# A decode-attention kernel: q's projection as a loop over the chunks of x, and eight unread matmuls in TensorE's waits

## The chip, the cores and the metric

The kernel runs on one core of a Trainium2 chip. The metric is the device time of one execution in microseconds (us); beside it stands the time of a profiled execution, whose trace is what the prediction reads. A core has TensorE (PE in the profile; its weight loads are PEld), VectorE (DVE), ScalarE (ACT), GpSimd (POOL) and SyncE (SP), each with a program of its own, and 16 DMA engines that all queues share. The engines wait for each other through semaphores, which are counters.

## The reference

Two attention layers A and B of one shape, each for one new token, and their outputs side by side. For each:

```python
q = (x @ wq).reshape(B, Sq, H, Dh).transpose(0, 2, 1, 3)     # x 1x1x512, wq 512x4096, H=32, Dh=128
scores = einsum("bhqd,bhkd->bhqk", q, k_cache) * Dh ** -0.5  # k_cache 1x32x8192x128, bf16
p = softmax(scores)
o = einsum("bhqk,bhkd->bhqd", p, v_cache)                    # v_cache 1x32x8192x128
out = o.transpose(0, 2, 1, 3).reshape(1, 1, 4096) @ wo       # wo 4096x512
```

K and V of both layers are 64 MiB each, 256 MiB together; with the weights 285 MB are read once.

## The kernel before, in words

**The rounds.** The 64 heads of both layers are worked on in N = 16 groups of G = 4 heads, one group a round. A group's K or V is 8 MiB. It is laid on 128 partitions, 32 partitions for each head and 256 positions on each partition. K has two slots in SBUF (`kn`), V has one (`vn`).

**SyncE issues all the large loads in one written order**, each behind a wait of its own: both `wq` (into the room of V, line 187), K of rounds 0 and 1 (line 197), V of round 0 (line 205), K of round 2, V of round 1, K of round 3 and so on. `load_v(0)` waits on `c_q` until all of q's matmuls have read `wq` (line 203). `load_v(n)` waits until round n-1 has read V (line 201). `load_k(n)` waits until TensorE has read K of round n-2 (line 196, semaphore `c_red`). The last two V come in two parts of 192 and 64 positions (line 207), with a semaphore for each. At the end come `wo` of A, the first half of `wo` of B, the last V, and the other half of `wo` of B in six pieces (`load_wob`, line 220).

**The projection q (lines 409 to 423).** `x` lies on the partitions in C = 4 chunks, and q is wanted on all partitions at once, so a chunk of `x`, repeated over 128 columns, is the stationary operand and 512 columns of `wq` move. Eight turns of a loop `r` make two groups each, `j` = 0 and 1, with one PSUM tile (`yps[0]`, `yps[1]`) for each. For a group TensorE waits until ScalarE has copied that tile's former content (`c_qa`), then issues four matmuls in a row, one for each chunk, and raises `c_q` once behind the fourth. ScalarE waits for that one (`w_q`) and copies four 32x128 pieces into `qmem` (line 372), while TensorE makes the other group.

**A round.** VectorE multiplies K by q in place, in two halves (line 280, `muls`); it begins only when all of q has been copied (line 273). TensorE sums over part of the head dimension with an identity matrix in four tiles (`scores`: a matmul of one element, line 430, that opens the tile, then a hardware loop of four turns with four matmuls each, line 436). VectorE sums the rest (line 308). Maximum, its spread and the exponentials follow on VectorE, TensorE and ScalarE (lines 313, 476, 478, 378, 383). When V has landed, 64 matmuls of 32x512 add up p times V in `acc` (line 492), and in the next round VectorE takes the diagonal out of `acc` (lines 285 and 288) and TensorE sums it over partitions (`total_of_group`, line 442).

**The end.** In the last two rounds the 64 matmuls wait a second time, ahead of the last 16, for the second part of V (`w_v2`, line 490). In the last round, `mid` (lines 447 to 467) multiplies what is known of the output by `wo`. Behind the rounds TensorE takes the pieces of `wo` of B as they land (line 506), with `total_of_group` for the last group ahead of the second piece; the sum is copied out by VectorE (line 352) and ScalarE (line 386), and sent to HBM.

Of the kernel before, what the change touches and what calls it, by code (L numbers as in the profile page):

```python
# [11 lines left out]
P = 128  # L12
# [33 lines left out]
def bass_concat_heads__mha_block_cached__gqa_block_cached__decode_kernel(  # L46
# [19 lines left out]
    H, Sk, Dh = ks[0].shape[1:]  # L66
# [3 lines left out]
    C = D // P  # L70
    scale = float(Dh) ** -0.5

    G = 4
# [4 lines left out]
    N = NA * GA  # L78
# [16 lines left out]
    with ExitStack() as st:  # L95
# [8 lines left out]
        vn = sb("vn", [P, KS], BF16)  # L104
# [12 lines left out]
        xT = sb("xT", [P, NA * C], BF16)  # L117
# [66 lines left out]
        @block.sync  # L184
        def _(e):
            for a in range(NA):
                e.dma_start(vn[:, a * WQ:(a + 1) * WQ],
                            wqs[a].rearrange("(p c) n -> p (c n)", p=P)).then_inc(s_w[a], 16)

            def group(x, n):  # L190
                a, i = divmod(n, GA)
                return x[a][0, G * i:G * (i + 1)].rearrange("h (p t) d -> (h p) (t d)", p=HP)

            def load_k(n):
                if n >= 2:
                    e.wait_ge(c_red, RED * (n - 1))
                e.dma_start(kn[:, n % 2 * KS:(n % 2 + 1) * KS], group(ks, n)).then_inc(s_k[n % 2], 16)

            def load_v(n):
                if n:  # L200
                    e.wait_ge(c_pv, n + 1)
                else:
                    e.wait_ge(c_q, N)
                if n < N - 2:
                    e.dma_start(vn[:], group(vs, n)).then_inc(s_v, 16)
                else:
                    for t0, t1, s in ((0, VT, s_v), (VT, T, s_v2)):
                        e.dma_start(vn[:, t0 * Dh:t1 * Dh],  # L208
                                    group(vs, n)[:, t0 * Dh:t1 * Dh]).then_inc(s, 16)

            def load_wob(g):
                h0, n, rows = WOB[g]
                src = wos[1][h0 * Dh:(h0 + n) * Dh, :]
                dst = kn[:, WO + h0 * NOUT:WO + (h0 + n) * NOUT]
                if rows:
                    src = src.rearrange("(p j) n -> p (j n)", p=P)
                elif n > 1:
                    src = src.rearrange("(j p) n -> p j n", p=P)
                    dst = dst.rearrange("p (j n) -> p j n", j=n)
                e.dma_start(dst, src).then_inc(s_wob[g], 16)  # L220

            load_k(0)
            load_k(1)
            for n in range(N - 1):
                load_v(n)
                if n + 2 < N:
                    load_k(n + 2)
            e.wait_ge(c_red, RED * (N - 1))
            e.dma_start(kn[:, 0:WO], wos[0].rearrange("(p j) n -> p (j n)", p=P)).then_inc(s_woa, 16)
            load_wob(0)  # L230
            load_v(N - 1)
            for g in range(1, len(WOB)):
                load_wob(g)
            e.wait_ge(s_out, 16)
# [120 lines left out]
        @block.scalar  # L355
        def _(e):
            with once(e):
                for a in range(NA):
                    e.dma_start(xrow[a:a + 1, :], xs[a][0]).then_inc(s_x, 16)
                w_q = _Stepped(e, c_q, 1, 1)  # L360
                w_bc = _Stepped(e, c_bc, 1, 1)
                w_nb = _Stepped(e, c_nb, 1, 1)
                w_pv = _Stepped(e, c_pv, 1, 1)
                e.wait_ge(c_pv, 1)
                e.copy(xT[:].rearrange("p (a c) -> p c a", c=C),
                       misc[:, 0:C * NA].rearrange("p (c a) -> p c a", a=NA)).then_inc(c_qa, 2)
                with e.Fori(0, N // 2) as r:
                    for j in range(2):
                        w_q()
                        for h in range(G):  # L370
                            p = slice(h * HP, (h + 1) * HP)
                            i = e.copy(qflat[p, bass.ds(r * (2 * Dh) + j * Dh, Dh)],  # L372
                                       yps[j][p, h * Dh:(h + 1) * Dh])
                        i.then_inc(c_qa, 1)
                e.wait_ge(c_pool, NPOOL)
                with e.Fori(0, N):
                    w_bc()
                    e.activation(negb[:], bmp[:, 0:G], AF.Copy, scale=-scale).then_inc(c_nb, 1)  # L378
                    w_nb()
                    w_pv()  # L380
                    for h in range(G):
                        p = slice(h * HP, (h + 1) * HP)
                        e.activation(pt[p, 0:T, h], s_sb[p, :], AF.Exp, bias=negb[p, h:h + 1], scale=scale,  # L383
                                     accum_out=rsum[p, h:h + 1]).then_inc(c_p, 4)
                e.wait_ge(c_y, 2)
                e.copy(out_sb[:, NH:NOUT], yps[1][HP:HP + NA, 0:NH]).then_inc(c_ya, 1)
                e.wait_ge(c_yd, 2)
                e.wait_ge(c_ya, 1)
                e.dma_start(out[0].rearrange("o (a n) -> (o a) n", a=NA), out_sb[:]).then_inc(s_out, 16)
# [3 lines left out]
        def _(e):  # L393
            with once(e):
# [14 lines left out]
                with e.Fori(0, N // 2) as r:  # L409
                    with e.If(r == GA // 2):  # L410
                        e.wait_ge(s_w[1], 16)
                    a = r // (GA // 2)
                    w0 = r * (2 * G * Dh) + a * (WQ - H * Dh)
                    x0 = a * C
                    for j in range(2):
                        e.wait_ge(c_qa, by_tile)
                        e.reg_add(by_tile, by_tile, 1)
                        for c in range(C):
                            i = e.matmul(  # L419
                                yps[j][:], xT[:, bass.ds(x0 + c, 1)].broadcast_to([P, P]),  # L420
                                vn[:, bass.ds(w0 + (c * H * Dh + j * G * Dh), G * Dh)],
                                start=(c == 0), stop=(c == C - 1))
                        i.then_inc(c_q, 1)

                def scores(tile):
                    e.wait_ge(c_mul, by_tile)
# [20 lines left out]
                def mid():  # L447
# [17 lines left out]
                    for b in range(2):  # L465
                        e.matmul(yps[1][b * HP:b * HP + NA, 0:NH], sel16[:, 0, 0:NA],
                                 yc[:, b * NH:(b + 1) * NH], start=True, stop=False, skip_group_check=True)

                with e.Fori(0, N) as r:
                    with e.Fori(0, NB // 2):  # L470
                        for tile in range(2):
                            scores(tile)
                            e.reg_add(koff, koff, HT * Dh - Dh)
                    e.reg_alu(koff, koff, 2 * KS - 1, op=ALU.bitwise_and)
                    e.wait_ge(c_g, by_round)
                    e.matmul(mtp[0:1, 0:P], m1[:], ident_f[:], start=True, stop=True).then_inc(c_gx, 1)  # L476
                    e.wait_ge(c_gm, by_round)
                    e.matmul(bmp[:, 0:G], ones_f[0:1, :], gm[:], start=True, stop=True).then_inc(c_bc, 1)  # L478
                    with e.If(r > 0):
                        total_of_group()  # L480
                    with e.If(r == N - 1):
                        mid()
                    e.wait_ge(c_p, by_round)
                    e.matmul(misc[:, 0:G], ones_f[:], rsum[:], start=True, stop=True)  # L484
                    e.wait_ge(s_v, by_round)
                    e.reg_add(by_round, by_round, 16)
                    for g in range(NG):
                        if g * W == VT:
                            with e.If(r >= N - 2):
                                w_v2()  # L490
                        k = g % G * HP
                        m = e.matmul(acc[k:k + HP, :], ptf[:, g * W * G:g * W * G + HP],  # L492
                                     vn[:, g * W * Dh:(g + 1) * W * Dh], start=(g < G), stop=(g >= NG - G))
                    m.then_inc(c_pv, 1)


                for g in range(1, len(WOB)):
                    h0, n, rows = WOB[g]
                    if g == 2:
                        total_of_group()  # L500
                    e.wait_ge(s_wob[g], 16)
                    if h0 == H - G:
                        e.wait_ge(c_o, N + 1)
                    for h in range(h0, h0 + n):
                        for b in range(2):
                            m = e.matmul(yps[1][b * HP:b * HP + NA, 0:NH], o2[:, H + h, :],  # L506
                                         wo_rows(H + h)[:, b * NH:(b + 1) * NH], start=False,
                                         stop=(h == H - 1), skip_group_check=True)
# [29 lines left out]
```

## Time and profile before

| | |
|---|---|
| runs | 665.43, 665.60, 665.69 us; median 665.6 |
| profiled execution | 665.7 us, span 664.2 us (1.5 us lie around the span) |
| busy time | PE 385.1 us, DVE 363.3 us, ACT 76.0 us |
| mean granted TensorE clock | 0.784 |
| read from HBM | 285.21 MB, 429 GB/s over the span |

A row of the timeline has start, duration, engine, source line, operation, output <- inputs, shape, count, and in brackets the idle time ahead with what ended it. SPq and ACTq are the queues that issue transfers. A chain row has start, duration and what the time went to; "DMA vn<-..." there is the time between a transfer's issue and its landing. PEclk is the granted clock of TensorE, where 1.00 is full speed.

### The profile page before, as it was taken

What the parts mean: (1) busy time and instruction counts of PE and PEld (TensorE: products, weight loads), DVE (VectorE), ACT (ScalarE), POOL (GpSimd) and SP (SyncE); (2) the same over time, 40 slices, a digit from 0 to 9 for tenths busy, and PEclk for the clock granted to TensorE, in tenths of its full rate; (3) what the DMA queues carried; (4) which work ended last, traced back from release to release, by engine and by line L of the source; (5) the groups of instructions that cost most, each with busy time, mean ns of one, the idle gap of its engine ahead of it and who ended that gap; (6) DMA issues with size and microseconds to landing.
All of it is one profiled execution on the core that took longest, in us unless ns stands there. A gap on an engine that the chain in (4) does not pass through costs nothing.

```text
span 664.2 us, 7946 instructions
## 1 busy us (share of the span) xinstructions
PE 385.1 (58%) x2398; PEld 169.4 (25%) x2398; DVE 363.3 (55%) x250; ACT 76.0 (11%) x211; POOL 2.3 (0%) x12
## 2 busy tenths in 40 slices
PE   1719392854819275481928548192854819285776
PEld 0203141322304132230413223041322304132332
DVE  1046757548292654829275482927547292754821
ACT  1710202020010202001020200102020010202020
POOL 1000000000000000000000000000000000000000
PEclk9968787786958778695877869597786959778789
DMA  9999999999999999999989999999999999989998
GB/s 379 442 442 442 442 442 391 430 442 442 442 442 399 422 442 442 442 442 442 442 387 434 442 442 442 442 442 414 406 442 442 442 442 442 434 387 458 426 413 344
DMA packets 6472, 285.22 MB, mean 429 GB/s; under 512 B 708, under 2 KB 1224, under 8 KB 1608
## 3 DMA queue, kind: packets, MB, share of 16 engines
q1 hardware_dynamic: 6464, 285.22, 99.5%
q10 hardware_dynamic: 8, 0.00, 0.0%
HBM read 285.21 MB, written 0.00 MB: 429 GB/s over the span
## 4 chain that ended last, share of the span: by engine, by line
DMA 82%; PE 15%; issue 1%; ACT 1%; SPq 0%; ACTq 0%; DVE 0%
DMA vn<-in_A_v_cache_dram 41%; DMA vn<-in_B_v_cache_dram 34%; PE acc L492 13%; DMA kn<-in_B_wo_dram 5%; PE yps L419 2%; DMA vn<-in_A_wq_dram 2%; ACT qmem L372 1%; SPq L220 0%; PE yps L506 0%; SPq L208 0%; ACTq L43 0%; ACTq L372 0%; DVE out_sb L352 0%
## 5 line engine op out<-in xcount | busy, mean ns | idle before, releaser
L280 DVE TENSOR_TENSOR kn<-kn,qmem 128x16384 bf16<-128x16384 bf16 x32 | 276.7, 8688 | 49.6 <-DMA kn<-in_A_k_cache_dram 37.1
L436 PE MATMUL rps<-kn,ident 128*128 x1024 | 236.2, 383 | 0.4
L492 PE MATMUL acc<-vn,pt 128*32 128x512 bf16 x1024 | 92.0, 537 | 153.5 <-DMA vn<-in_A_v_cache_dram 80.4
L308 DVE TENSOR_REDUCE s_sb<-rps 128x64 f32<-128x512 f32 x64 | 44.3, 692 | 166.8 <-PE rps L436 166.8
L436 PEld LDWEIGHTS rps<-kn,ident 128*128 128x128 bf16 x1024 | 96.5, 98 | 110.4 <-issue 22.3
L492 PEld LDWEIGHTS acc<-vn,pt 128*32 128x32 bf16 x1024 | 38.4, 129 | 200.6 <-issue 194.3
L378 ACT ACTIVATE negb<-bmp 128x4 f32<-128x4 f32 x16 | 2.8, 173 | 547.3 <-PE bmp L478 547.3
L383 ACT ACTIVATE pt<-s_sb,negb 32x256 bf16<-32x256 f32 x64 | 54.9, 858 | 4.3 <-ACT negb L378 3.0
L484 PE MATMUL misc<-rsum,ones_f 128*128 128x4 f32 x32 | 9.2, 358 | 56.4 <-ACT pt L383 56.4
L285 DVE TENSOR_SCALAR om<-acc,msk 128x128 f32<-128x128 f32 x16 | 5.6, 350 | 41.8 <-PE acc L492 41.8
L484 PEld LDWEIGHTS misc<-rsum,ones_f 128*128 128x128 f32 x32 | 7.8, 304 | 58.2 <-ACT pt L383 57.7
L419 PE MATMUL yps<-vn,xT 128*128 x64 | 17.4, 422 | 8.5 <-ACT qmem L372 4.4
L288 DVE SCALAR_TENSOR_TENSOR om<-acc,msk,om 128x128 f32<-128x128 f32 x48 | 16.8, 351 | 5.9
L430 PE MATMUL rps<-ones_bf,zrow 1*128 1x1 bf16 x64 | 11.0, 172 | 15.6 <-DVE kn L280 15.4
L476 PE MATMUL mtp<-ident_f,m 128*1 128x128 f32 x32 | 6.1, 270 | 22.6 <-DVE m L313 22.6
L372 ACT CAST qmem<-yps 32x128 f32 x64 | 16.4, 256 | 9.4 <-PE yps L419 8.6
L430 PEld LDWEIGHTS rps<-ones_bf,zrow 1*128 1x128 bf16 x64 | 5.8, 91 | 42.8 <-issue 42.8
L383 ACT ACTIVATION_READ_ACCUMULATOR pt<-s_sb,negb 32x1 f32 x64 | 15.9, 248 | 0.0
L419 PEld LDWEIGHTS yps<-vn,xT 128*128 x64 | 6.6, 103 | 18.9 <-issue 16.0
L478 PE MATMUL bmp<-gm,ones_f 1*128 1x4 f32 x32 | 6.1, 258 | 7.3 <-DVE gm L315 7.3
L297 DVE TENSOR_TENSOR oD<-mtp,rinv 128x4 f32 x15 | 2.4, 162 | 13.6 <-PE mtp L442 13.6
L315 DVE TENSOR_REDUCE gm<-mtp 1x4 f32<-1x128 f32 x16 | 4.5, 279 | 8.9 <-PE mtp L476 8.9
(56 smaller groups left out, 50.9 us busy)
## 6 DMA issues: line engine op xcount, KB each, us to landing
vn<-in_B_v_cache_dram SPq DMA_DIRECT2D x2, 6144.0 KB, 28.0
vn<-in_A_wq_dram SPq DMA_DIRECT2D x1, 4096.0 KB, 12.2
vn<-in_B_wq_dram SPq DMA_DIRECT2D x1, 4096.0 KB, 21.4
vn<-in_B_v_cache_dram SPq DMA_DIRECT2D x2, 2048.0 KB, 32.5
kn<-in_A_wo_dram SPq DMA_DIRECT2D x1, 4096.0 KB, 27.8
kn<-in_B_wo_dram SPq DMA_DIRECT2D x1, 2048.0 KB, 32.3
kn<-in_B_wo_dram SPq DMA_DIRECT2D x3, 512.0 KB, 34.1
kn<-in_B_wo_dram SPq DMA_DIRECT2D x1, 256.0 KB, 35.2
```

The lines of the kernel that those rows point to most:

```text
L280: e.tensor_tensor(k, k, qflat[:, bass.ds(q, Dh)].unsqueeze(1).broadcast_to([P, HM, Dh]), ALU.mult).then_inc(c_mul, 2)
L288: e.scalar_tensor_tensor(om[t % 2][:], acc[:, t * Dh:(t + 1) * Dh], msk[:, t:t + 1], om[(t + 1) % 2][:], ALU.mult, ALU.add).then_inc(*((c_ ...
L308: e.tensor_reduce(s_sb[:, h * HT:(h + 1) * HT], rps[:, h % 2, :].rearrange("p (t d) -> p t d", d=DW), AX.X, ALU.add).then_inc(c_sr, 1)
L372: i = e.copy(qflat[p, bass.ds(r * (2 * Dh) + j * Dh, Dh)], yps[j][p, h * Dh:(h + 1) * Dh])
L383: e.activation(pt[p, 0:T, h], s_sb[p, :], AF.Exp, bias=negb[p, h:h + 1], scale=scale, accum_out=rsum[p, h:h + 1]).then_inc(c_p, 4)
L419: i = e.matmul(yps[j][:], xT[:, bass.ds(x0 + c, 1)].broadcast_to([P, P]), vn[:, bass.ds(w0 + (c * H * Dh + j * G * Dh), G * Dh)], start=(c ...
L430: e.matmul(rps[:, tile, 0:1], zrow[:], ones_bf[0:1, 0:1], start=True, stop=False, skip_group_check=True)
L436: m = e.matmul(ro, ident[:], src, start=False, stop=False, skip_group_check=True)
L476: e.matmul(mtp[0:1, 0:P], m1[:], ident_f[:], start=True, stop=True).then_inc(c_gx, 1)
L478: e.matmul(bmp[:, 0:G], ones_f[0:1, :], gm[:], start=True, stop=True).then_inc(c_bc, 1)
L484: e.matmul(misc[:, 0:G], ones_f[:], rsum[:], start=True, stop=True)
L492: m = e.matmul(acc[k:k + HP, :], ptf[:, g * W * G:g * W * G + HP], vn[:, g * W * Dh:(g + 1) * W * Dh], start=(g < G), stop=(g >= NG - G))
```

## The change

Two things. **q's matmuls**: the four chunks no longer stand in a row for one group. First both tiles are waited for and opened with a matmul of one element that writes zeros (stationary `zrow`). Then a hardware loop over the four chunks issues one matmul for each of the two groups, each of which raises `c_q`. So `c_q` counts 64 instead of 16, group 0 is complete at the seventh of eight and group 1 at the eighth, and ScalarE and SyncE wait for these counts. **Eight matmuls that nobody reads**: `turn_over(n)` issues n matmuls of 128x128 by 128x512 into the scores tile `rps[:, 0]`, in a hardware loop. It stands with n = 5 ahead of the wait for the second part of V in each of the last two rounds, and with n = 3 ahead of the last `total_of_group`.

```diff
-                    e.wait_ge(c_q, N)
+                    e.wait_ge(c_q, N * C)
...
-                w_q = _Stepped(e, c_q, 1, 1)
+                w_q = _Stepped(e, c_q, 2 * C - 1, 2 * C)
+                w_q2 = _Stepped(e, c_q, 2 * C, 2 * C)
...
-                        w_q()
+                        (w_q, w_q2)[j]()
...
-                        for c in range(C):
-                            i = e.matmul(
-                                yps[j][:], xT[:, bass.ds(x0 + c, 1)].broadcast_to([P, P]),
-                                vn[:, bass.ds(w0 + (c * H * Dh + j * G * Dh), G * Dh)],
-                                start=(c == 0), stop=(c == C - 1))
-                        i.then_inc(c_q, 1)
+                        e.matmul(yps[j][:, 0:1], zrow[:], ones_bf[0:1, 0:1], start=True, stop=False,
+                                 skip_group_check=True)
+                    with e.Fori(0, C) as c:
+                        for j in range(2):
+                            e.matmul(yps[j][:], xT[:, bass.ds(x0 + c, 1)].broadcast_to([P, P]),
+                                     vn[:, bass.ds(w0 + c * (H * Dh) + j * G * Dh, G * Dh)],
+                                     start=False, stop=False, skip_group_check=True).then_inc(c_q, 1)
...
+                def turn_over(n):
+
+                    with e.Fori(0, n):
+                        e.matmul(rps[:, 0, :], ident[:], vn[:, 0:512], start=True, stop=True)
+
...
                             with e.If(r >= N - 2):
+                                turn_over(5)
                                 w_v2()
...
                     if g == 2:
+                        turn_over(3)
                         total_of_group()
```

## The prediction

> **What bounds the kernel now.** I read the page first, its DMA queues.
>
> ```profile
> span 664.2 us, 7946 instructions
> ...
> PE 385.1 (58%) x2398; PEld 169.4 (25%) x2398; DVE 363.3 (55%) x250; ACT 76.0 (11%) x211; POOL 2.3 (0%) x12
> ...
> q1 hardware_dynamic: 6464, 285.22, 99.5%
> ```
>
> The large loads keep the 16 DMA engines occupied for 99.5% of the span, while the busiest compute engine, TensorE, is busy for 385.1 of 664.2 us. Next I read the chain of work that ended last, in order of time. It runs through V alone, but its starts are landings of V, and these tell the pace.
>
> ```profile
> 35.61 45.11 DMA vn<-in_A_v_cache_dram
> 80.72 0.12 issue
> ...
> 119.42 0.12 issue
> ...
> 584.11 0.12 issue
> ...
> 626.38 35.17 DMA kn<-in_B_wo_dram
> 661.55 0.04 issue
> 661.59 0.64 PE yps L506 x6
> ...
> 662.59 0.41 DVE out_sb L352
> ```
>
> V of round 0 lands at 80.72 and V of round 1 at 119.42, 38.70 later; V of round 13 lands at 584.11, and (584.11 - 80.72) / 13 = 38.72 us a round: the pace is steady. Each round moves a K and a V, so 8 MiB take 19.36 us. The kernel is a single file of transfers from start to end, and only 1.5 us of compute stand behind the last landing (661.55 to 663.0). Hence the rule for this change: a delay of compute costs nothing while the file has work, and every microsecond in which the file runs dry is added to the end, since no later stage goes faster than the file.
>
> **The place where the file could run dry.** For that I read the timeline of the first round and two rows on the first load.
>
> ```profile
> 0.80 0.37 SPq L187 DMA_DIRECT2D vn<-in_A_wq_dram  x1
> ...
> 13.85 5.98 PE L419 MATMUL yps<-vn,xT 128*128 x16 [4.16 <-DMA vn<-in_A_wq_dram]
> ...
> 20.54 1.90 PE L419 MATMUL yps<-vn,xT 128*128 x8 [0.71 <-ACT qmem L372]
> ...
> 21.71 2.14 ACT L372 CAST qmem<-yps 32x128 f32 x8 [0.48 <-PE yps L419]
> ...
> 23.17 1.90 PE L419 MATMUL yps<-vn,xT 128*128 x8 [0.73 <-ACT qmem L372]
> ...
> 34.85 2.14 ACT L372 CAST qmem<-yps 32x128 f32 x8 [0.48 <-PE yps L419]
> ...
> 42.16 17.29 DVE L280 TENSOR_TENSOR kn<-kn,qmem 128x16384 bf16<-128x16384 bf16 x2 [37.12 <-DMA kn<-in_A_k_cache_dram]
> ...
> 68.25 0.33 SPq L197 DMA_DIRECT2D kn<-in_A_k_cache_dram  x1
> ```
>
> ```profile
> vn<-in_A_wq_dram SPq DMA_DIRECT2D x1, 4096.0 KB, 12.2
> ```
>
> q is complete at 34.85 + 2.14 = 36.99. VectorE starts on K of round 0 at 42.16, when K has landed, so q is 5.1 us early. From that start to the issue of K of round 2 are 68.25 - 42.16 = 26.09 us. The file at that time holds V of round 0, which lands at 80.72. How early must the next load be issued? The first load had an empty file: issued at 0.80, landed 12.2 us later, of which 4 MiB at the pace above are 9.7 us; so an issue into an empty file costs about 2.5 us. K of round 2 is in time if issued by 80.72 - 2.5 = 78.2, that is 10.0 us later than now. Together with the 5.1 us, q may end about 15.1 us later, at 52.1, before the file runs dry. V of round 0 has more room: K of round 1 lands at 80.72 - 19.36 = 61.4, its issue may move from 35.61 to 58.9. PV of round 0 waits for V until 80.72, and V of round 1 is issued behind it with K of round 2 in the file ahead; that has room too.
>
> **q's loop, step by step.** Before, a turn takes 23.17 - 20.54 = 2.63 us, and ScalarE's eight copies (2.14) are 81% of it: while it copies group 0, TensorE makes group 1. After, group 0 is complete only at the seventh matmul of eight, and the next turn's loop can begin only when group 1 has been copied. So matmuls and copies stand one behind the other. The parts of a turn:
> - copy done to first matmul: group 0's four copies end at 21.71 + 1.07 = 22.78, the matmul starts at 23.17: 0.39. Of the opening matmul and the loop's entry I know this from the scores:
>
> ```profile
> 50.99 0.16 PE L430 MATMUL rps<-ones_bf,zrow 1*128 1x1 bf16 x1 [15.41 <-DVE kn L280]
> ...
> 51.22 6.02 PE L436 MATMUL rps<-kn,ident 128*128 x16
> ```
>
> The first half of the multiplication ends at 42.16 + 8.65 = 50.81, the opening matmul starts 0.18 later, the loop's first matmul 0.23 later: 0.41. So opening and loop entry fit in the same 0.4; I keep 0.39.
> - three iterations of the loop (two matmuls each) up to the seventh matmul, its duration, and ScalarE's start. A matmul lasts 0.38 and follows the one ahead at (1.90 - 0.38) / 7 = 0.217; group 0's fourth ended at 20.54 + 3 x 0.217 + 0.38 = 21.57 and the copy began at 21.71: 0.14.
> - eight copies, 2.14.
>
> The sum is 0.39 + 0.38 + 0.14 + 2.14 = 3.05 us and three iterations. What is an iteration? No such loop is in the trace. Below, it can't be less than two matmuls at 0.217, or 0.43. Above, the nearest row is the scores' loop with four matmuls a turn and an address calculation for each, as here:
>
> ```profile
> 601.05 0.55 PEld L436 LDWEIGHTS rps<-kn,ident 128*128 128x128 bf16 x4
> 601.92 0.55 PEld L436 LDWEIGHTS rps<-kn,ident 128*128 128x128 bf16 x4 [0.33 <-issue]
> 602.82 0.55 PEld L436 LDWEIGHTS rps<-kn,ident 128*128 128x128 bf16 x4 [0.35 <-issue]
> ```
>
> Its turns start 0.87 and 0.90 apart, where the matmuls alone would take 4 x 0.217 = 0.87: the sequencer, which reads and issues the instructions, is just about the bound. With half the matmuls and the whole cost of the back edge, a turn of the new loop lies between 0.43 and 0.90; I take the middle, 0.67. A turn of q then takes 3.05 + 2.01 = 5.06 us.
>
> [...]
>
> **The clock.** The first turns run at half speed, as the starts of weight loads show; and the clock falls when TensorE rests.
>
> ```profile
> 14.68 0.15 PEld L419 LDWEIGHTS yps<-vn,xT 128*128 x1 [0.28 <-issue]
> 15.11 0.15 PEld L419 LDWEIGHTS yps<-vn,xT 128*128 x1 [0.28 <-issue]
> ```
>
> ```profile
> 35.60:39.00 3.40, 0.00 (x0) 0.00 (x0) 0.00 (x0) 1.32 (x6) 0.00 (x0) 1.00 1.07 463
> 39.00:51.20 12.20, 0.16 (x1) 0.10 (x1) 9.04 (x2) 0.00 (x0) 0.00 (x0) 0.50 1.07 462
> 51.20:56.00 4.80, 4.79 (x12) 1.85 (x13) 4.80 (x1) 0.00 (x0) 0.00 (x0) 0.50 0.98 423
> ...
> 654.90:657.00 2.10, 0.04 (x4) 0.00 (x0) 0.00 (x0) 0.00 (x0) 0.00 (x0) 1.00 0.97 406
> ```
>
> At half clock matmuls start 0.43 apart. After 3.4 us without work the clock went to 0.50; it came back after 4.8 us of unbroken matmuls; a pause of 2.1 us did not lower it. At half clock a turn of the new loop is 3.05 + 3 x 0.86 and 0.2 for the longer matmul, 5.83. It offers 3.4 us of matmuls and then a pause of 2.4, less than what brought the clock back here, so I count three turns at half clock and five at full clock, in which the pause of about 2.8 us lies between the 2.1 and the 3.4 seen.
>
> [...]
>
> **The sum.** The first turn: 13.85 + 0.23 + 3 x 0.86 + 0.6 + 0.14 + 2.14 = 19.5. Two more turns at half clock, 11.7, and five at full clock, 25.3: q ends at 56.5 instead of 37.0. V of round 0 is issued at about 54.3, before 58.9. VectorE starts at 56.6 instead of 42.16, K of round 2 is issued 14.4 us later, at 82.7, and 78.2 would have been in time: 4.5 us of an idle file. In the rounds that follow nothing else is late: K of round 3 was issued at 102.1 and has until V of round 1 lands.
>
> **The eight unread matmuls.** Rows of the end:
>
> ```profile
> 618.13 5.94 PE L492 MATMUL acc<-vn,pt 128*32 128x512 bf16 x64 [6.07 <-DMA vn<-in_B_v_cache_dram]
> ```
>
> ```profile
> 657.06 1.05 PE L492 MATMUL acc<-vn,pt 128*32 128x512 bf16 x16 [2.12 <-DMA vn<-in_B_v_cache_dram]
> ...
> 659.99 0.38 PE L442 MATMUL mtp<-selh,om 128*128 128x4 f32 x2 [1.12 <-DVE om L288]
> ...
> 661.59 0.96 PE L506 MATMUL yps<-kn,o 128*2 128x256 bf16 x8 [0.15 <-DMA kn<-in_B_wo_dram]
> ```
>
> Five cost 5 x 0.217 = 1.1 us at full clock, up to 2.2 at half. In round 14 the 64 matmuls run almost through (5.94 us), so there is no wait to fill: scores of round 15 begin 1.1 to 2.2 us later, and V of round 15, issued behind them at 624.1, has `wo` ahead of it in the file. In the last round the wait is 2.12 us and covers five. Three, 0.7 us, lie in the wait of 1.12. Behind it TensorE waits for pieces of `wo` again (the last 0.15), so a delay of a few tenths is caught by the transfers. And the clock is at 1.00 there already. Gain nothing; cost 0 to 0.5, taken as 0.1.
>
> Together 4.6 us: 665.7 + 4.6 = 670.3 against the profiled execution's own time, which is 0.1 above the median of the runs. I keep **670.3 us**.
>
> **The rivals.**
> - **Hidden**: the loop runs at the matmuls' pace and the clock is up from the second turn. A turn is 3.05 + 1.3 = 4.35, q ends at 19.5 + 7 x 4.35 = 50.0, before 52.1. For it: matmuls elsewhere run back to back. Against: the scores' loop shows the sequencer near its bound. 665.7; the eight matmuls cost nothing. Chance 0.19, for all that gives less than 1.3 us.
> - **Half clock throughout**: bursts with pauses never bring the clock back, or the loop's turn costs 0.9 us, which gives about the same. q ends at 19.5 + 7 x 5.83 = 60.3; K of round 2 is issued at 86.5, 8.3 us too late: 674. For it: 4.8 us of unbroken work were needed to bring the clock back. Against: the pauses are shorter than 3.4 us. Chance 0.20.
> - **Faster**: the unread matmuls hold the clock up for the closing matmuls. Were it down at 657, the 16 matmuls of round 15 and the 32 on `wo` would take up to twice their time, and the 1.1 us behind the last landing as well; a kernel that is down in its usual run would gain 1.4 us or more. It decides if the clock falls in the pause of 2.1 us, and in this execution it doesn't (1.00). 664.2; chance 0.03.
>
> **How the numbers follow.** The forecast, a loss between 1.3 and 7 us, has 0.58. A measurement of this kernel tells apart about 0.2%, or 1.3 us. Below is the faster rival, 0.03; within is the hidden one, 0.19; the rest, 0.78, is slower. The range goes from the hidden case, 665.6, to the one at half clock, 674.2, and leaves out the faster case and part of that one.
>
> **What would show it.** Turns of q about 5 us apart, with ScalarE's copies behind the matmuls; VectorE's first multiplication released by q's copies near 56 instead of by K; K of round 2 issued after 80; V of round 0 still at 80.7, V of round 1 at about 124 and from there 38.7 a round. It is wrong if q ends before 52, if TensorE's clock stays low to the end of q, or if later V land closer than 38.7 apart, which would mean that the file can catch up.

## The result, and the profile after

The changed kernel takes 679.95 us (five runs, 679.68 to 681.47) against 665.63 of the kernel before in the same comparison: a ratio of 1.0216, with a 95% interval of 1.0206 to 1.0227. The prediction said slower, 670.3, with a range to 674.2. The sign was right; the loss is 14.3 us instead of 4.6. The profiled execution has a span of 678.5 us and a time of 679.95.

The page of the changed kernel, its slices and its DMA queue:

```profile
span 678.5 us, 8136 instructions
...
DMA  9997959999999999999999999999999999999998
GB/s 371 440 437 297 433 212 437 437 440 437 433 440 437 433 433 433 437 433 433 433 433 433 433 433 433 433 433 433 433 433 433 433 433 433 433 433 410 426 434 337
...
q1 hardware_dynamic: 6464, 285.22, 97.5%
```

A slice is 17 us. Two of them, the fourth and the sixth, have gaps (297 and 212 GB/s beside some 435), and no later one does (the lower numbers of the last slices stand in the kernel before as well, 413 and 344 there): the file of transfers ran dry twice within the first 102 us and never again. The timeline shows the two late issues, and who made them late:

```profile
64.05 2.14 ACT L373 CAST qmem<-yps 32x128 f32 x8 [4.47 <-PE yps L423]
64.37 0.33 SPq L205 DMA_DIRECT2D vn<-in_A_v_cache_dram  x1
66.72 17.29 DVE L280 TENSOR_TENSOR kn<-kn,qmem 128x16384 bf16<-128x16384 bf16 x2 [61.68 <-ACT qmem L373]
...
92.81 0.33 SPq L197 DMA_DIRECT2D kn<-in_A_k_cache_dram  x1
```

q is complete at 64.05 + 2.14 = 66.19, where it was at 36.99. VectorE now waits for q instead of K. V of round 0 is issued at 64.37, past the 58.9 up to which it would have been free. It lands 21.8 us later, at 86.2 instead of 80.72, which is the first gap. K of round 2 is issued at 92.81 instead of 68.25, which is the second. The distance from VectorE's start to that issue is 92.81 - 66.72 = 26.09 us, exactly that of before. What K of round 2 is late by, 92.81 - 78.2 = 14.6, is both gaps together, and appears in the chain, in the landing of V of round 1:

```profile
105.07 28.97 DMA vn<-in_A_v_cache_dram
134.04 0.12 issue
...
172.74 0.12 issue
...
598.46 0.12 issue
...
675.93 0.60 PE yps L515 x6
```

134.04 - 119.42 = 14.62. From there V lands every (598.46 - 134.04) / 12 = 38.70 us as before, and the end stands 14.34 us later than before (675.93 against 661.59). All of the loss is made before 105 us, and none of it comes back.

The loop that makes q late, in one turn of eight (PEld rows are the weight loads, two for each turn of the hardware loop):

```profile
24.56 2.14 ACT L373 CAST qmem<-yps 32x128 f32 x8 [4.45 <-PE yps L423]
...
26.83 0.16 PE L419 MATMUL yps<-ones_bf,zrow 1*128 1x1 bf16 x1 [0.92 <-ACT qmem L373]
27.39 0.22 PEld L423 LDWEIGHTS yps<-vn,xT 128*128 x2 [0.50 <-issue]
...
28.36 0.24 PEld L423 LDWEIGHTS yps<-vn,xT 128*128 x2 [0.75 <-issue]
...
29.39 0.24 PEld L423 LDWEIGHTS yps<-vn,xT 128*128 x2 [0.79 <-issue]
30.38 0.24 PEld L423 LDWEIGHTS yps<-vn,xT 128*128 x2 [0.74 <-issue]
31.13 1.06 ACT L373 CAST qmem<-yps 32x128 f32 x4 [4.42 <-PE yps L423]
```

The loop's turns start 0.97, 1.03 and 0.99 us apart, and a turn of q takes 31.13 - 24.56 = 6.57 us; before, it took 2.63. The loop's turn is the same at either clock (in the rows of windows the third number from the end is the granted clock):

```profile
47.15 0.60 PE L423 MATMUL yps<-vn,xT 128*128 x2 [0.43 <-issue]
48.12 3.04 PE L423 MATMUL yps<-vn,xT 128*128 x6 [0.37 <-issue]
...
53.70 0.24 PEld L423 LDWEIGHTS yps<-vn,xT 128*128 x2 [0.48 <-issue]
54.67 0.29 PEld L423 LDWEIGHTS yps<-vn,xT 128*128 x2 [0.74 <-issue]
```

```profile
47.00:48.00 1.00, 0.60 (x2) 0.19 (x2) 0.00 (x0) 0.00 (x0) 0.00 (x0) 1.00 0.00 0
...
54.00:55.00 1.00, 1.00 (x3) 0.21 (x2) 0.00 (x0) 0.00 (x0) 0.00 (x0) 0.50 0.00 0
```

At 1.00 the two matmuls are done in 0.60 us and TensorE then idles until the next turn, 0.97 us after the start of this one; at 0.50 the next turn starts after 0.97 us too.

### The profile page after: what moved, and what is told of

It reads as the page before. It is cut to its first block, busy times and chain, and to the rows that moved or that the text cites. A ratio compares the mean times of both kernels' runs of the same rounds, so it can differ in the third digit from the quotient of the medians.

```text
span 678.5 us, 8136 instructions
## 1 busy us (share of the span) xinstructions
PE 398.8 (59%) x2417; PEld 170.5 (25%) x2427; DVE 362.6 (53%) x250; ACT 76.0 (11%) x211; POOL 2.3 (0%) x12
## 4 chain that ended last, share of the span: by engine, by line
DMA 74%; PE 18%; issue 2%; ACT 2%; DVE 2%; ACTq 0%; SPq 0%; DVEq 0%
DMA vn<-in_B_v_cache_dram 34%; DMA vn<-in_A_v_cache_dram 33%; PE acc L500 11%; DMA kn<-in_B_wo_dram 5%; PE yps L423 4%; PE rps L438 2%; DMA vn<-in_A_wq_dram 2%; ACT qmem L373 1%; DVE kn L280 1%; ACT pt L384 0%; ACTq L373 0%; PE yps L419 0%; SPq L220 0%; SPq L208 0%; PE yps L515 0%
## 5 line engine op out<-in xcount | busy, mean ns | idle before, releaser
L438 PE MATMUL rps<-kn,ident 128*128 x1024 | 239.4, 386 | 1.0
L500 PE MATMUL acc<-vn,pt 128*32 128x512 bf16 x1024 | 85.2, 504 | 138.7 <-DMA vn<-in_B_v_cache_dram 75.8
L500 PEld LDWEIGHTS acc<-vn,pt 128*32 128x32 bf16 x1024 | 35.5, 122 | 179.3 <-issue 169.9
L423 PE MATMUL yps<-vn,xT 128*128 x64 | 30.1, 580 | 4.9 <-issue 4.8
L419 PE MATMUL yps<-ones_bf,zrow 1*128 1x1 bf16 x16 | 2.5, 159 | 17.2 <-ACT qmem L373 13.2
```

Of the source, the lines that this page charges most:

```text
L423: e.matmul(yps[j][:], xT[:, bass.ds(x0 + c, 1)].broadcast_to([P, P]), vn[:, bass.ds(w0 + c * (H * Dh) + j * G * Dh, G * Dh)], start=False, ...
L438: m = e.matmul(ro, ident[:], src, start=False, stop=False, skip_group_check=True)
```

## The experiments

The theory to test had two halves. First, only the time in which the file of transfers is empty counts; it begins when K of round 2 is issued after 78.2. Second, q is late because TensorE's sequencer needs 1.0 us for a turn of the new loop, whatever the clock. The rivals: the order of the matmuls (copies behind them instead of beside them), the half clock, the back edge of the loop (its jump to the next turn), and the unread matmuls. A time that stands without a ratio is that of one execution.

**Each part alone.** The change without the eight unread matmuls (q's loop alone), and the kernel before with them alone:

```diff
-                                turn_over(5)
...
-                        turn_over(3)
```

> The changed kernel without the eight unread matmuls, q's loop as changed. Theory (all of the loss comes from q): 679.5 to 680.5 us, as the whole change. Rival (the unread matmuls delay the end too): more than 1 us below the whole change.

Measured: 680.4 us; ratio 1.0219, 1.0204 to 1.0235, that of the whole change. All of the loss is q's.

> The kernel before with the eight unread matmuls alone. Theory (they lie in waits or are caught by the file of transfers): 665.4 to 666.2 us, within 0.1% of before. Rival (they delay the last round): 667 us or more; rival (they hold the clock up): 664.5 us or less.

Measured: ratio 1.0028, 1.0015 to 1.0041; times from 666.31 to 669.32, median 668.44. More than the theory allowed, but the span of its profiled execution is 664.1 us, 0.1 less than before. Inside the span the matmuls cost nothing: V of round 13 lands at 584.01, before at 584.11. The extra lies around the span, 668.84 - 664.1 = 4.7 us where it was 1.5. The DMA view of the last 4 us of the span and the 6 behind it shows what is new:

```profile
q8 instruction: 1, 0.02, 0.6%
q14 instruction: 1, 0.01, 0.2%
```

One more fetch of instructions, 0.02 MB, behind the last work. In the kernel before and in the changed one this window has the q14 line alone of the two. Two more runs ask whether it is the size of TensorE's program. One has the five matmuls without the three:

> The kernel before with the five unread matmuls of the last two rounds alone, without the three at the end, so that TensorE's program grows by half as much as with both. With both, the span was 664.1 us as before, but the time 668.4, and the trace had one more fetch of instructions behind the last work. Theory (the extra time is that fetch, and it comes when TensorE's program passes a size): no such fetch, 665.4 to 666.2 us. Rival (the five matmuls themselves cost it): 667 us or more.

Measured: 665.59 us, ratio 0.9996, 0.9987 to 1.0005: five matmuls cost nothing. Half of the expectation missed: the profiled execution, at 666.84 the longest of eleven, does have the q8 line; the ten others took 665.41 to 665.91. The other run has matmuls that never run:

```diff
+                            with e.If(e.snap(by_round) >= 4096):
+                                for _ in range(5):
+                                    e.matmul(rps[:, 0, :], ident[:], vn[:, 0:512], start=True, stop=True)
```

> The kernel before with five matmuls behind a condition that never holds, so that TensorE's program is as long as with both unread groups, but does nothing more than before. Theory (a fetch of instructions that comes with the size of the program): the fetch is in the trace, the span stays at 664 to 665 us and the time is 666.3 to 669.5 us. Rival (the unread matmuls cost it by running): 665.4 to 666.2 us.

Measured: ratio 1.0061, 1.0047 to 1.0075, times of 666.84 to 671.05, span 664.0, and in the window around the end:

```profile
q8 instruction: 1, 0.02, 0.7%
q14 instruction: 1, 0.01, 0.3%
```

Instructions that never run cost at least as much as the unread matmuls, so it isn't the running of these that costs. A longer program fits as the cause; the condition that this run adds to each round was not tested apart from it. The changed kernel has both additions and no such fetch in its profiled execution (679.95 - 678.5 = 1.45). That its loop makes q's part of the program shorter would fit, but isn't shown. What brings the fetch on, and why the time varies from run to run of one program (666.31 to 669.32 us with the unread matmuls, 666.84 to 671.05 with those that never run), isn't settled. Size alone can't decide it: two runs further below, with 35 and with 50 unread matmuls ahead of q, differ only in the count of a loop (and ran on two chips), and the profile of the first has the q8 line (667.26 - 664.7 = 2.6) where that of the second has none (1.5).

**Order or loop.** The loop over the chunks written out, in the same order:

```diff
-                    with e.Fori(0, C) as c:
+                    for c in range(C):
```

> The changed kernel with the loop over the chunks written out: the same opening matmuls, the same order of the eight matmuls, no hardware loop around them. Theory (TensorE's sequencer is the bound of the new loop: a turn costs 1.0 us whatever the clock): matmuls come at the clock's pace, 0.22 to 0.43 us apart, a turn of q falls from 6.56 us to between 4.4 and 6.0, q ends between 50 and 62 and the time lies between 666 and 675 us. Rival (the order is what costs, copies behind matmuls): a turn stays above 6.2 us and the time at 678 to 680 us.

Measured: 673.66 us; ratio 1.0109, 1.0086 to 1.0131. q ends at 58.43. The matmuls now come at the clock's pace:

```profile
31.42 0.16 PE L419 MATMUL yps<-ones_bf,zrow 1*128 1x1 bf16 x1 [0.92 <-ACT qmem L373]
31.78 3.19 PE L423 MATMUL yps<-vn,xT 128*128 x8 [0.20 <-issue]
...
37.31 1.41 PEld L423 LDWEIGHTS yps<-vn,xT 128*128 x8 [0.30 <-issue]
```

The second row is a turn at half clock (its weight loads from 32.63 to 33.91 start 0.43 us apart); in the third, eight weight loads (PEld) in 1.41 us are the pace of full clock, with addresses from registers as in the loop. So reading an address from a register costs no time here; the turns take 4.45 us (full clock) to 5.94 (half). Order and half clock together move q's end by 21.4 us (58.43 - 36.99), the loop by the other 7.8; of the loss they make 8.0 us (673.66 against 665.64), the loop the other 6.3. The order, the larger part, the prediction counted. The half clock it counted for three turns of eight only, while here a single turn takes as little as 4.45 us. Seven turns at full clock behind the first would end q near 17.35 + 2.14 + 7 x 4.45 = 50.6 (an estimate from this run's rows), so some 7.8 us of the 21.4 are the clock's.

**What a turn of the loop costs.** The loop with fixed addresses (it reads one chunk and the first columns each time):

```diff
-                    with e.Fori(0, C) as c:
+                    with e.Fori(0, C):
                         for j in range(2):
-                            e.matmul(yps[j][:], xT[:, bass.ds(x0 + c, 1)].broadcast_to([P, P]),
-                                     vn[:, bass.ds(w0 + c * (H * Dh) + j * G * Dh, G * Dh)],
+                            e.matmul(yps[j][:], xT[:, 0:1].broadcast_to([P, P]),
+                                     vn[:, j * G * Dh:(j + 1) * G * Dh],
```

> The changed kernel with the loop kept, but each matmul in it reads a fixed address: every turn takes the first chunk of x and the first columns of wq, so q is not x @ wq here. Theory (the sequencer's time goes into the arithmetic for the addresses): pairs of matmuls start 0.43 us apart at full clock and 0.86 at half clock instead of 1.0, and the time falls to 666 to 674 us. Rival (the back edge of a hardware loop costs it): pairs stay 0.9 to 1.0 us apart and the time at 678 to 680 us.

Measured: 670.02 us. At full clock the pairs start 0.40 to 0.44 apart:

```profile
51.76 0.12 PEld L423 LDWEIGHTS yps<-vn,xT 128*128 128x128 bf16 x2
52.20 0.12 PEld L423 LDWEIGHTS yps<-vn,xT 128*128 128x128 bf16 x2 [0.33 <-issue]
52.60 0.14 PEld L423 LDWEIGHTS yps<-vn,xT 128*128 128x128 bf16 x2 [0.29 <-issue]
```

The back edge is in this loop too, so it isn't what makes 1.0 us: the address arithmetic adds the other 0.6. To add arithmetic without addresses, 14 steps a turn that nothing uses (on top of the fixed addresses; the register's set-up isn't shown):

```diff
+                        for _ in range(7):
+                            e.reg_add(idle, idle, 5)
+                            e.reg_alu(idle, idle, 255, op=ALU.bitwise_and)
```

> The run with fixed addresses in q's loop, with 14 steps of register arithmetic a turn added that nothing uses; q isn't x @ wq here either. Theory (a loop turn is the back edge, about 0.4 us, and the arithmetic ahead of its matmuls): pairs of matmuls start 0.9 to 1.2 us apart at any clock, against 0.40 with the fixed addresses alone, and the time is 677 to 684 us. Rival (it is the matmuls' reading of addresses from registers, or something else of the loop): pairs stay 0.4 to 0.86 apart and the time at 669 to 672 us.

Measured: 708.32 us, and pairs 1.80 apart:

```profile
35.09 0.14 PEld L428 LDWEIGHTS yps<-vn,xT 128*128 128x128 bf16 x2 [1.41 <-issue]
36.89 0.14 PEld L428 LDWEIGHTS yps<-vn,xT 128*128 128x128 bf16 x2 [1.66 <-issue]
38.69 0.14 PEld L428 LDWEIGHTS yps<-vn,xT 128*128 128x128 bf16 x2 [1.67 <-issue]
```

The direction is the theory's, the size isn't: (1.80 - 0.40) / 14 = 0.10 us a step, about twice what I had counted on, and pairs and time lie above the ranges given. The address arithmetic of the changed kernel is only three instructions a turn (its profile has 8136 instructions, that with fixed addresses 8040: 96 more in 32 turns), so one of these costs about 0.2 us. Why it costs twice a plain step wasn't tested.

The clock was the next rival: five more unread matmuls in each turn, while ScalarE copies.

```diff
+                    for _ in range(5):
+                        e.matmul(rps[:, 0, :], ident[:], ptf[:, 0:512], start=True, stop=True)
```

> The changed kernel with five more unread matmuls behind the loop of each turn of q, while ScalarE copies, so that TensorE's clock stays up. Theory (the sequencer is the bound of the new loop): pairs of matmuls still start 1.0 us apart, a turn takes 6.2 to 6.6 us, 678 to 680 us. Rival (half clock is what made the loop longer than forecast): pairs 0.45 to 0.7 apart, a turn about 5 us, 669 to 672 us.

Measured: 683.62 us, above the range given; 4.7 us of it lie around the span (678.9), with a q8 line at the end. In the turn shown the clock is up, and the loop no shorter:

```profile
34.10:37.60 3.50, 2.23 (x8) 0.81 (x9) 0.00 (x0) 0.00 (x0) 0.00 (x0) 1.00 0.99 431
```

```profile
34.16 0.23 PEld L423 LDWEIGHTS yps<-vn,xT 128*128 x2 [0.49 <-issue]
35.16 0.23 PEld L423 LDWEIGHTS yps<-vn,xT 128*128 x2 [0.78 <-issue]
36.14 0.23 PEld L423 LDWEIGHTS yps<-vn,xT 128*128 x2 [0.75 <-issue]
```

At a granted clock of 1.00, in a window with 2.23 us of matmuls in 3.5, the turns are still 1.0 us apart. The half clock is out as the cause of the 1.0 us. Last, the overlap given back, with twice as many loop turns:

```diff
-                w_q = _Stepped(e, c_q, 2 * C - 1, 2 * C)
+                w_q = _Stepped(e, c_q, C, 2 * C)
...
                     for j in range(2):
...
-                    with e.Fori(0, C) as c:
-                        for j in range(2):
+                        with e.Fori(0, C) as c:
```

> The changed kernel with the loop over the chunks inside each group: four turns of one matmul for group 0, then four for group 1, so that ScalarE copies one group while TensorE makes the other, as before the change, but with all address arithmetic in a loop. Theory (the sequencer is the bound): twice as many loop turns of 0.7 to 0.9 us each, a turn of q takes 6.5 to 8 us in spite of the overlap, and the time is 679 to 690 us. Rival (the lost overlap is the main cost): a turn falls to 3 to 4.5 us and the time to 665.5 to 667 us.

Measured: 695.46 us (2.9 around the span), a turn of q 8.2 us, both somewhat above the ranges given.

```profile
30.63 0.10 PEld L422 LDWEIGHTS yps<-vn,xT 128*128 x1 [0.49 <-issue]
31.47 0.10 PEld L422 LDWEIGHTS yps<-vn,xT 128*128 x1 [0.74 <-issue]
32.32 0.10 PEld L422 LDWEIGHTS yps<-vn,xT 128*128 x1 [0.75 <-issue]
```

A loop turn with one matmul costs 0.85 us here, not much less than one with two. With such a loop the overlap doesn't pay: ScalarE's copies are hidden, and the eight loop turns for two groups take more time than that saves.

**What a late q costs.** The kernel before, with 50, 100 or 35 unread matmuls ahead of q:

```diff
+                with e.Fori(0, 50):
+                    e.matmul(rps[:, 0, :], ident[:], vn[:, 0:512], start=True, stop=True)
                 with e.Fori(0, N // 2) as r:
```

> The kernel before with 35 unread matmuls ahead of q. With 50 of them a matmul took 0.41 us and q ended at 56 us; with 35 it should end near 50 us and K of round 2 be issued near 76, about 2 us before the 78.2 that the two larger doses confirm. Theory (only the time in which the file is empty counts): 665.4 to 666.2 us. Rival (any delay past K's landing at 42 us costs something): 667 to 673 us.

> The kernel before with 50 unread matmuls ahead of q, so that q ends about 12 us later, near 49 us, short of the 52.1 us at which the file of transfers would run dry. Theory (only the time in which the file is empty counts): 665.4 to 666.2 us. Rival (each microsecond by which q ends later than K's landing at 42 counts): 671 to 673 us.

> The kernel before with 100 unread matmuls ahead of q: q ends near 60 us, K of round 2 is issued near 86 us. Theory (only the time in which the file is empty counts): 7 to 8.5 us are lost, 672.5 to 674.5 us. Rival (a gap of the file is caught up later): 666 to 669 us. Rival (all of the delay counts from 42 us on): 682 to 685 us.

Measured: 666.27 us (ratio 1.0009, 0.9999 to 1.0018), 670.03 (1.0063, 1.0046 to 1.0079) and 690.03 (1.0361, 1.0343 to 1.0378). The two larger doses turned out larger than I had counted on, since a matmul in a loop of its own took 0.41 us and not 0.22; their times miss the ranges given. The smallest is 0.07 above its range in the median, with V of round 1 on time. The rule they test stands, as the table shows (us; issues from the timeline, landings from the chain; the three runs that change nothing up to the end of q are left out, since it ends there within 0.4 us of before):

| run | q ends | K of round 2 issued | past 78.2 | V of round 1 later than 119.42 |
|---|---|---|---|---|
| before | 36.99 | 68.25 | no | 0 |
| 35 ahead of q | 49.95 | 76.58 | no | 0.07 |
| fixed addresses | 55.96 | 82.58 | 4.4 | 4.25 |
| 50 ahead of q | 56.06 | 82.85 | 4.65 | 4.70 |
| written out | 58.43 | 85.20 | 7.0 | 8.23 |
| five more in each turn | 65.53 | 92.73 | 14.5 | 14.40 |
| q's loop alone | 66.01 | 93.17 | 15.0 | 14.92 |
| changed kernel | 66.19 | 92.81 | 14.6 | 14.62 |
| 100 ahead of q | 76.44 | 103.40 | 25.2 | 25.24 |
| overlap given back | 80.02 | 106.65 | 28.45 | 28.24 |
| 14 steps added | 92.93 | 119.55 | 41.35 | 41.26 |

q may end 13 us later at no cost, and from 78.2 on every microsecond counts once. One row is off by 1.2, the loop written out; there a q8 fetch of instructions lies between 70 and 100 us, beside the load of K of round 2, which took 23.1 us from issue to landing instead of 21.9. That the fetch caused it is argued, not shown.

## Why the prediction was wrong

**Right: the frame.** The file of transfers as the bound, the place where it runs dry and the limit of 78.2 held in all eleven rows of the table, within 0.25 us but for the one named; the 26.09 us from VectorE's start to the issue came again in the changed kernel. Later V land 38.70 apart, as said. An issue into an empty file was taken as 2.5 us; K of round 2 landed 21.9 us after its issue, 2.5 more than 19.36. One sign failed with q's end: V of round 0 did not land at 80.7, since its issue came past the 58.9 that the prediction itself had worked out.

**Wrong: "a turn of the new loop lies between 0.43 and 0.90; I take the middle, 0.67".** It measured 1.0, above the upper bound. The bound took the scores' loop, which has four matmuls a turn, for the dearer one. But what a turn costs is mostly the arithmetic for the addresses, 0.6 of the 1.0 us, not the matmuls: the scores step one register by constants, while q's loop works its addresses out of the chunk's number anew in each turn (`x0 + c`, `w0 + c * (H * Dh)`), and with fixed addresses the turn fell to 0.40, matmuls and back edge together. Three turns ahead of the seventh matmul cost 2.99 us instead of 2.01.

**Wrong: "opening and loop entry fit in the same 0.4".** From the copies' end at 24.56 + 2.14 = 26.70 to the first weight load at 27.39 are 0.69 us, because the same arithmetic stands ahead of the first matmul: with fixed addresses they are 0.22 (49.39 + 2.15 = 51.54 to 51.76). The scores' entry, 0.23, was again the row of a loop with less of it.

**Wrong: "three turns at half clock and five at full clock".** In windows of one microsecond the granted clock was 0.50 from 21 to 24, from 28 to 31 and from 35 to 38, in the middle of the bursts of matmuls, and 1.00 in the pauses between these; from 51 to 66 it stayed at 0.50. It fell although the pauses between bursts were about 2.6 us (28.37 + 2.99 = 31.36 to 33.96), with two matmuls of one element inside them. In the changed kernel this hardly shows, since a turn of the loop takes 1.0 us at either clock. With the loop written out it does, as said above: there q ended at 58.43, two microseconds past the forecast, although the loop cost nothing.

**Sizes.** A turn is 0.69 + 2.99 + 0.75 + 2.14 = 6.57 us, where 5.83 was forecast at half clock and 5.06 at full. The first turn adds little (its copies end at 17.97 + 2.14 = 20.1 against 19.5); the seven others took 46.1 us against 37.0: q ends 9.7 us later than forecast, and K of round 2 is issued 10.1 later (VectorE starts 0.53 us behind q, where 0.1 was taken). Of the 9.7 us the iterations make 5.7 (seven times 2.99 against two times 2.58 and five times 2.01), the loop's entry 2.1, the way from the seventh matmul to the copies (0.75 against 0.52, or 0.72 at half clock) 1.2, and the first turn 0.6. That is the miss: a loss of 14.3 us instead of 4.6. The rival "half clock throughout, or the loop's turn costs 0.9 us" was nearest with 674, and it too kept the short loop entry.

**Right, but by half: the unread matmuls.** In the changed kernel they lie in the waits, as the timeline of the end shows:

```profile
671.39 1.05 PE L500 MATMUL acc<-vn,pt 128*32 128x512 bf16 x16 [1.59 <-DMA vn<-in_B_v_cache_dram]
...
673.14 0.82 PE L474 MATMUL rps<-vn,ident 128*128 128x512 bf16 x3
...
674.32 0.39 PE L444 MATMUL mtp<-selh,om 128*128 128x4 f32 x2 [0.37 <-DVE om L288]
```

The last wait for V is 1.59 us beside them, and 0.37 of the wait for `om` is left over. What the prediction never asked is whether the added instructions could cost anything outside the span; in the kernel before they would, by the 1.9 us of the ratio 1.0028.

## What to carry to other kernels

Ask of a kernel that its transfers bound when the next load must be issued, and a delay has a price: nothing up to that time, and then one for one (here 0.07 us for an issue at 76.58, and 25.24 for one that came 25.2 past 78.2). Ask of a new order what ran beside what: copies that stand behind the matmuls instead of beside them were, with the clock, the larger part of q's delay (21.4 of 29.2 us). A short hardware loop on TensorE paid for its address arithmetic in each turn (1.0 us for two matmuls, 0.40 with fixed addresses), and with one matmul of fixed addresses a turn took 0.41 us where matmuls in a row start 0.22 apart; where the result is waited for, write the matmuls out (673.66 us here instead of 679.95), or step a register by a constant (that was not tried for q; the scores' loop does so, at 0.87 to 0.90 us for four matmuls). And look at the time around the span as well as at the span: a longer program can, it seems, cost where no instruction shows it (five matmuls that never run: a ratio of 1.0061, with a span of 664.0).

## What the runs showed of the hardware

A loop of one matmul with fixed addresses took 0.41 us a turn at a granted clock of 1.00 (50 in 20.48 us), where matmuls in a row start 0.22 us apart. What of the 0.41 is the back edge, no run shows.

A plain register step on TensorE's sequencer took 0.10 us, in a loop turn with 14 of them: (1.80 - 0.40) / 14.

An additional fetch of instructions (the q8 line, 0.02 MB) around the end of the span goes with 1.0 to 3.2 us more around the span (2.5, 2.6, 2.8, 2.9, 3.1, 4.7 and 4.7 us in the seven profiled executions that have it, 1.4 to 1.7 in the seven that don't). Of 43 executions of the kernel before, five have 2.3 to 2.7 as well (time less span); whether by such a fetch, no profile shows.
